# A Fourier filter and gated network on one core: the second transform stage as three products, with its input stored as a high and a low part

## The chip, the cores and the metric

The kernel runs on one core of a Trainium2 chip. The metric is the device time of one execution in microseconds (us). One core has TensorE (PE, matrix products), VectorE (DVE), ScalarE (ACT), GpSimd (POOL) and SyncE (SP, which here only issues transfers). PE, DVE, ACT, POOL and SP each work through a list of instructions in a fixed order; the order is the one in which the program was written.

## The reference

```python
X = np.fft.rfft(x, axis=1)                       # x: 8 x 3136 x 256
Y = X * (filt_r + 1j * filt_i)[None]
h0 = np.fft.irfft(Y, n=3136, axis=1)
h = np.maximum(h0 @ w_in, 0)                     # 256 -> 1024
c = sum(conv_w[k] * shift(h, k - 1) for k in range(3))   # three taps along the sequence
out = (h * sigmoid(c)) @ w_out                   # 1024 -> 256
```

All of it in fp32; the weights w_in, conv_w and w_out come as float64 bits and are turned into fp32 on the chip.

## The kernel before

**Arithmetic.** A matrix product with fp32 operands can be written as one fp32 matmul, or as three matmuls of the type fp32r on operands that were split into a rounded high part and a low remainder: high by high, high by low, low by high. The helper `mm3` (L186 to L189) writes the three. The network's products (`inner`, `project`) are such triples; the Fourier transforms use single fp32 matmuls.

**Transforms.** 3136 = 112 x 28. A batch goes through four stages, each in 14 pieces q of two columns (112 or 120 partitions x 512 values). Stage "1" (`by_column`, L245) reads x, multiplies by a table `tab`, and its result goes through a copy of ACT (`store`, L240, tile `st`) to DRAM, `a_dram`. Stage "2" (`second`, L249, L252 for q = 13) reads `a_dram` back in another order into a tile `tin` and multiplies by the constant `s2_sb`; `filt` then multiplies by the filter on DVE (L264 to L266) and adds on POOL (L267). Stage "3" (L249 again, input `z`) multiplies by `s3_sb` and goes through ACT and `st` to `b_dram`. Stage "4" (L275) reads `b_dram` into `tin`; DVE and ACT write it to the network's input `y`, ACT the high part (L156), POOL the low part (L162).

**Loop.** Batch 0 is transformed by other code in the first 86 us. Then comes the main loop over slots m: 8 slots (NF) make a unit of 510 tokens, and 48 slots make about a batch. In each slot, in this order of writing: every eighth time the finished output of a unit is copied out by DVE (`evacuate`, L549; counted within a batch of slots these are slots 6, 14, 22, 30, 38 and 46); `from_bank` for the transforms of the slot before; `want_in`, which issues input loads on SP; `transform` for this slot's transforms; `inner` (six 512-column matmuls, L187 to L189); ACT's relu, centre (L500), sigmoid, rounding; DVE's first tap (L504), gate (L510), second tap (L504); POOL's remainder of the gate (`rest_g`, L162); `project` (twelve 256-column matmuls, L536 to L538). ACT's centre writes one of four `t` buffers, which POOL's remainder frees.

**Plan of the transforms.** A table built ahead (`plan`) says which transforms stand in which slot. Counted from its own start, the t-th stretch of 48 slots (t = 1 to 7) holds stages "2", "3" and "4" of batch t and stage "1" of batch t + 1. The first stretch is special: slots 0 to 5 hold two "1" each, those of batch 1 that are still missing. From the second stretch on, "2" stands in slots 2, 3, 5, 7, 9, 11, 12, 14, 16, 18, 20, 21, 23, 25, "3" three slots after its "2", "1" in slots 0, 1, 4, 6, 8, 10, 13, 22, 27, 29 to 32 and 45, and "4" in slots 33 to 44, two of them in 33 and 39. The last stretch has no "1".

**Buffers and queue.** Two PSUM banks (`ps_t`) are shared by all transforms of the loop, in turn, so that a transform waits until the transform before the last has left its bank. A bank is left when ACT has copied it ("1", "3"), when DVE's `filt` has read it ("2"), or when DVE has copied it ("4"). `tin` has five buffers for all kinds of input, `st` three. `want_in` runs up to five inputs ahead. SP issues nearly all transfers: for each slot the stores of the slot before, then new loads of `tin`, then tables and filters.

Of the kernel before, what the change touches and what calls it, by code (L numbers as in the profile page):

```python
# [9 lines left out]
F32 = mybir.dt.float32  # L10
# [8 lines left out]
N2 = 28  # L19
G = 28  # L20
# [112 lines left out]
def tile_fft_filter_gated_ffn(  # L133
# [57 lines left out]
    dram = ctx.enter_context(tc.tile_pool(name="dram", bufs=1, space=bass.MemoryType.DRAM))  # L191
    a_dram = [dram.tile([N2, 112, D], F32, name=f"a_dram{b}") for b in range(B)]
    b_dram = [dram.tile([N2, 112, D], F32, name=f"b_dram{b}") for b in range(B)]
    a_out = [t[:].rearrange("n p d -> p n d") for t in a_dram]
    a_in = [t[:].rearrange("n (r g) d -> (n r) g d", g=G) for t in a_dram]
    b_out = [t[:].rearrange("n (r g) d -> (n r) g d", g=G) for t in b_dram]
# [5 lines left out]
    s2_sb = wc.tile([112, 120], F32, name="s2_sb")  # L202
    s2s_sb = wc.tile([112, 120], F32, name="s2s_sb")
    s3_sb = wc.tile([120, 112], F32, name="s3_sb")
    s3s_sb = wc.tile([120, 112], F32, name="s3s_sb")
    one_sb = wc.tile([128, 128], F32, name="one_sb")
    cw = wc.tile([128, 3, NF], F32, name="cw")
# [24 lines left out]

    def load_in(pool, kind, b, q, bufs, tag):
        r = pool.tile([112, 2, D], F32, name=tag, bufs=bufs)
        nc.sync.dma_start(out=r, in_={"1": xv, "2": a_in, "4": b_in}[kind][b][:, pair(q)])
        return r

    def store(pool, kind, b, q, ps, bufs, tag, queue=nc.sync):
        st = pool.tile([112, 2, D], F32, name=tag, bufs=bufs)
        nc.scalar.activation(st, ps[0:112].rearrange("p (j d) -> p j d", d=D), AF.Copy)  # L240
        queue.dma_start(out={"1": a_out, "3": b_out}[kind][b][:, pair(q)], in_=st)

# [11 lines left out]
    def second(ps, q, r):  # L254
        by_row(ps[0:120], q, r, s2_sb, s2s_sb)

    def third(ps, q, z):
# [27 lines left out]
    def load_weights(k, pool):  # L285
        raws[k] = raw = pool.tile([128, 2, 1024], I32, name="raw", bufs=1 if pool is tp else 2)
        for part, w in enumerate((w_in, w_out)):
            nc.sync.dma_start(out=raw[:, part], in_=w[:, 1024 * k:1024 * k + 1024])
# [6 lines left out]

    def convert(k, pool, n=2):

        for j in range(2):
            em = pool.tile([128, 2, 2, 256], I32, name="em", bufs=n)
            w = pool.tile([128, 2, 256], F32, name="ws", bufs=n)  # L300
            yield from to_f32(w, raws[k][:, :, 512 * j:512 * j + 512], em[:, 0], em[:, 1])
# [10 lines left out]
    with (  # L312
# [3 lines left out]
    ):  # L316
        fts, tabs, rows, zs, pss = {}, {}, {}, {}, {}
        by_r = [sc.tile([120, 4, N2], F32, name=f"by_r{i}", bufs=1) for i in range(2)]
        bt = sc.tile([128, KT, G, 112], F32, name="bt", bufs=1)
# [31 lines left out]
        with tc.tile_pool(name="sq", bufs=2) as sq:  # L351
# [15 lines left out]
            def first_loads(c):  # L367
                table("1", c)
                r = sq.tile([128, 4, D], F32, name="rows", bufs=5)
                nc.sync.dma_start(out=r, in_=xt[0:128, 4 * c:4 * c + 4])  # L370
# [24 lines left out]
            for i in range(NP + 4):  # L395
# [6 lines left out]
                if 0 <= i - NP < AHEAD:  # L402
                    ps = bank()
                    by_column(ps, tab("1", i - NP), rows.pop(("1", i - NP)))
                    store(tp, "1", 1, i - NP, ps, 3, "st", nc.scalar)
                if 0 <= i - 4 < NP:
# [7 lines left out]
                if i == 5:  # L414
                    table("1", 0)
                    for q in range(AHEAD):
                        r = sq.tile([128, 2, D], F32, name="xa", bufs=2)
                        nc.sync.dma_start(out=r, in_=xt[N1:N1 + 128, pair(q)])
# [33 lines left out]
    ts, hs, gs, pos, joined = {}, {}, {}, {}, {}  # L452
    ring = [[wp.tile([128, UO + 66], F32R, name=f"g{i}{h}", bufs=1) for h in range(2)] for i in range(4)]
    for pair_of in ring:
# [176 lines left out]
    def transform(op):  # L631
# [20 lines left out]
    def from_bank(op):  # L652

        kind, b, q = op
        ps = banks.pop(op)
        if kind in "13":
            store(tp, kind, b, q, ps, 3, "st")
            stored[kind, b] = stored.get((kind, b), 0) + 1
# [15 lines left out]
    with tc.manual_schedule(engines=COMPUTE | {mybir.EngineType.SP}):  # L674
# [3 lines left out]
        want_filter(0)  # L678
        late = convert(3, wp, 1)
        for m in range(NF * NU + PLAG + 1):  # L680
            p1, p2, p3, p4, p6, p7 = (at(m - k) for k in (1, 2, 3, 4, PLAG, PLAG + 1))
            new, old = plan.get(m, []), plan.get(m - 1, [])
            if p7:
                evacuate(*p7)
            for op in old:
                from_bank(op)
# [73 lines left out]
```

## Time and profile before

| | |
|---|---|
| median of 3 runs | 1554.89 us (1553.32 to 1556.66) |
| the profiled execution | 1554.59 us |
| its span in the profile | 1552.8 us |
| busy: PE, DVE, ACT, POOL | 98%, 76%, 74%, 53% of the span |
| moved by DMA | 229.49 MB, mean 148 GB/s |

Line numbers (L249) are those of the kernel before. "Idle before, releaser" in a group of instructions is the time in which the engine stood still ahead of them, and what it was waiting for. An fp32 matmul counts as several instructions of PE ("x2" for one piece of stage "2"). Ends of matmuls are modelled; the distance from one start to the next tells their cost better than their busy time. The chain of waits gives each step the time to the next step.

### The profile page before, as it was taken

The numbers are of one execution on the slowest core, as the hardware profiler recorded it, in microseconds if no ns is written. First come the engines' busy times: TensorE is split into PE (matmuls) and PEld (weight loads), VectorE is DVE, ScalarE is ACT, GpSimd is POOL, SyncE is SP. The second block draws the span as 40 slices with busy tenths as digits, with TensorE's granted clock in tenths as the row PEclk, the third lists the DMA queues.
The fourth block names the chain that finished last, engine by engine and source line by source line (L and its number), as shares of the span: only waits on it lengthen the run. The fifth ranks groups of instructions, "written<-read, shape, count | busy, mean of one in ns | idle before, by whom it ended". The sixth has DMA issues, their size and how long they took to land.

```text
span 1552.8 us, 26446 instructions
## 1 busy us (share of the span) xinstructions
PE 1519.7 (98%) x9202; PEld 1290.6 (83%) x9202; DVE 1185.3 (76%) x1810; ACT 1144.7 (74%) x1973; POOL 828.3 (53%) x721
## 2 busy tenths in 40 slices
PE   6999999999999999999999999999999999999999
PEld 5777788877997789877898778987799878999998
DVE  7978766788677877778777776778867888777776
ACT  3576668766896668866787667976688667888886
POOL 4644447545574555645565445744557445664444
PEclk9999999999999999999999999999999999999999
DMA  8867653665436555465544665356543543300000
GB/s 302 256 185 215 208 170 109 181 200 166 135 110 202 179 155 159 121 193 169 177 124 143 185 196 153 97 179 203 165 135 100 160 140 110 101 28 15 28 28 30
DMA packets 158436, 229.49 MB, mean 148 GB/s; under 512 B 16432, under 2 KB 109088, under 8 KB 158304
## 3 DMA queue, kind: packets, MB, share of 16 engines
q1 hardware_dynamic: 157824, 227.35, 48.4%
q8 instruction: 73, 1.20, 0.3%
q14 instruction: 59, 0.48, 0.1%
q10 hardware_dynamic: 480, 0.46, 0.1%
HBM read 157.10 MB, written 70.65 MB: 147 GB/s over the span
## 4 chain that ended last, share of the span: by engine, by line
PE 92%; DVE 2%; ACT 2%; DMA 2%; issue 2%; SPq 0%; POOL 0%; ACTq 0%; POOLq 0%; DVEq 0%
PE ps_h L187 12%; PE ps_h L189 12%; PE ps_h L188 12%; PE po L536 12%; PE po L538 12%; PE po L537 11%; PE ps_t L249 10%; PE ps_t L275 6%; PE ps_t L245 5%; DMA rows<-in_x 1%; PE ps_t L252 1%; ACT br L346 0%; DVE v L265 0%; DVE z L264 0%; DMA f<-in_filt 0%
## 5 line engine op out<-in xcount | busy, mean ns | idle before, releaser
L504 DVE SCALAR_TENSOR_TENSOR t<-ps_h,cw,t 128x510 f32<-128x510 f32 (+1 forms) x800 | 589.1, 737 | 301.5 <-ACT t L500 298.4
L162 POOL TENSOR_TENSOR g<-t,g 128x510 fp32r<-128x510 f32 (+1 forms) x400 | 505.3, 1273 | 203.6 <-ACT g L156 191.9
L536 PE MATMUL po<-wo,g 128*128 128x256 f32 (+1 forms) x1576 | 440.4, 279 | 0.1
L538 PE MATMUL po<-wo,g 128*128 128x256 f32 (+1 forms) x1576 | 439.5, 279 | 0.0
L537 PE MATMUL po<-wo,g 128*128 128x256 f32 (+1 forms) x1576 | 439.3, 279 | 0.0
L495 ACT ACTIVATE ps_h<-ps_h 128x512 f32<-128x512 f32 (+1 forms) x400 | 234.7, 587 | 243.9 <-PE ps_h L189 242.2
L500 ACT ACTIVATE t<-ps_h,cw 128x510 f32<-128x510 f32 (+1 forms) x400 | 272.4, 681 | 102.8 <-POOL g L162 70.1
L267 POOL TENSOR_TENSOR z<-z,v 120x512 f32<-120x512 f32 x112 | 144.8, 1293 | 380.4 <-DVE v L266 312.7
L187 PE MATMUL ps_h<-y,wi 128*128 128x512 f32 (+1 forms) x688 | 333.4, 485 | 0.5 <-DVE y L159 0.5
L536 PEld LDWEIGHTS po<-wo,g 128*128 128x128 f32 (+1 forms) x1576 | 297.0, 188 | 17.3 <-ACT g L156 0.3
L537 PEld LDWEIGHTS po<-wo,g 128*128 128x128 f32 (+1 forms) x1576 | 296.4, 188 | 17.0
L538 PEld LDWEIGHTS po<-wo,g 128*128 128x128 f32 (+1 forms) x1576 | 296.6, 188 | 0.6 <-POOL g L162 0.5
L189 PE MATMUL ps_h<-y,wi 128*128 128x512 f32 (+1 forms) x688 | 270.1, 393 | 0.0
L188 PE MATMUL ps_h<-y,wi 128*128 128x512 f32 (+1 forms) x688 | 270.1, 393 | 0.0
L510 DVE TENSOR_TENSOR t<-ps_h,t 128x510 f32<-128x510 f32 (+1 forms) x400 | 268.6, 671 | 0.9 <-ACT t L507 0.8
L507 ACT ACTIVATE t<-t 128x510 f32<-128x510 f32 (+1 forms) x400 | 245.3, 613 | 1.7 <-DVE t L504 1.6
L156 ACT ACTIVATE g<-t 128x510 fp32r<-128x510 f32 (+1 forms) x400 | 245.1, 613 | 0.2 <-DVE t L510 0.2
L162 POOL TENSOR_TENSOR y<-z,y 128x448 fp32r<-128x448 f32 x98 | 138.5, 1422 | 93.8 <-ACT y L156 91.9
L187 PEld LDWEIGHTS ps_h<-y,wi 128*128 128x128 f32 x688 | 130.4, 189 | 44.3 <-issue 23.6
L188 PEld LDWEIGHTS ps_h<-y,wi 128*128 128x128 f32 x688 | 130.7, 190 | 41.3 <-issue 24.3
L189 PEld LDWEIGHTS ps_h<-y,wi 128*128 128x128 f32 x688 | 130.0, 189 | 30.2 <-POOL wi L162 0.3
L240 ACT ACTIVATE st<-ps_t 112x512 f32<-112x512 f32 x194 | 114.0, 590 | 11.2 <-PE ps_t L245 11.1
(91 smaller groups left out, 1608.0 us busy)
## 6 DMA issues: line engine op xcount, KB each, us to landing
filt<-in_filt SPq DMA_DIRECT2D x98, 512.0 KB
tin<-a_dram SPq DMA_DIRECT2D x98, 224.0 KB
b_dram<-st SPq DMA_DIRECT2D x98, 224.0 KB
tin<-b_dram SPq DMA_DIRECT2D x98, 224.0 KB
tin<-in_x SPq DMA_DIRECT2D x96, 224.0 KB
a_dram<-st SPq DMA_DIRECT2D x96, 224.0 KB
out<-ot SPq DMA_DIRECT2D x45, 256.0 KB
tab<-in_m SPq DMA_DIRECT2D x98, 98.0 KB
```

What stands on the lines that cost most here:

```text
L156: nc.scalar.activation(dst, src, AF.Copy)
L162: nc.gpsimd.tensor_tensor(out=dst, in0=src, in1=hi.bitcast(F32), op=ALU.subtract)
L187: nc.tensor.matmul(ps, lhsT=wh, rhs=rh, start=start, stop=False, **kw)
L188: nc.tensor.matmul(ps, lhsT=wh, rhs=rl, start=False, stop=False, **kw)
L189: nc.tensor.matmul(ps, lhsT=wl, rhs=rh, start=False, stop=stop, **kw)
L500: nc.scalar.activation(t, hs[u, f][:, 1:n + 1], AF.Copy, scale=cw[:, 1, f:f + 1])
L504: nc.vector.scalar_tensor_tensor(out=t, in0=h[:, k:place(u)[2] + k], scalar=cw[:, k, f:f + 1], in1=t, op0=ALU.mult, op1=ALU.add)
L507: nc.scalar.activation(ts[u, f], ts[u, f], AF.Sigmoid)
L510: nc.vector.tensor_mul(ts[u, f], hs.pop((u, f))[:, 1:place(u)[2] + 1], ts[u, f])
L536: nc.tensor.matmul(o, lhsT=gh[:, c:c + n], rhs=wo[0][:, f], start=first, stop=False, skip_group_check=True)
L537: nc.tensor.matmul(o, lhsT=gh[:, c:c + n], rhs=wo[1][:, f], start=False, stop=False, skip_group_check=True)
L538: nc.tensor.matmul(o, lhsT=gl[:, c:c + n], rhs=wo[0][:, f], start=False, stop=last, skip_group_check=True)
```

## The change

**Stage "2" of batches 2 to 7 becomes a triple.** The constants `s2_sb` and `s2s_sb` are split once, at slot 8, by POOL, into `second_parts` (tiles `s20`, `s21`, `s2s0`, `s2s1`). `second_split` runs `mm3` on them. Batch 1 keeps the single fp32 matmul.

**Stage "1" of batches 2 to 7 stores two parts.** ACT writes the rounded high part to the tile `sh`, as it wrote `st`; DVE then subtracts it from the bank and writes the low part right behind (L159, 112 x 512). Both go to DRAM, the low part to a new tensor `r_dram`, and are loaded back by two loads for each piece of stage "2", into the two halves of a tile `tia`. That makes 84 subtractions, 84 more stores and 84 more loads of 224 KB.

**Buffers.** `tin` (now for "1" and "4" only) has three buffers instead of five; `tia` (stage "2") has three, twice as large; `st` (stage "3") two instead of three; `sh` (stage "1") two. `want_in` runs up to six inputs ahead, but has at most three of stage "2" and three of the others loaded and unused. The `rows` tiles of batch 0 have four buffers instead of five, and the last quarter of the weights passes through buffers of `tia` and `st`. The network's `ring` tiles are narrower by 64 columns that nothing uses.

```diff
-    def load_in(pool, kind, b, q, bufs, tag):
-        r = pool.tile([112, 2, D], F32, name=tag, bufs=bufs)
-        nc.sync.dma_start(out=r, in_={"1": xv, "2": a_in, "4": b_in}[kind][b][:, pair(q)])
+    def load_in(pool, kind, b, q):
...
+        if kind == "2":
+            r = pool.tile([112, 2, 2, D], F32R, name="tia", bufs=3)
+            for h, t in enumerate((a_in, r_in)):
+                nc.sync.dma_start(out=r[:, h].bitcast(F32), in_=t[b][:, pair(q)])
+            return r
+        r = pool.tile([128, 2, D], F32, name="tin", bufs=3)[0:112]
+        nc.sync.dma_start(out=r, in_={"1": xv, "4": b_in}[kind][b][:, pair(q)])
         return r
...
+    def store_first(pool, b, q, ps, queue=nc.sync):
+
+        st = pool.tile([112, 2, 2, D], F32R, name="sh", bufs=2)
+        p = ps[0:112].rearrange("p (j d) -> p j d", d=D)
+        hi_act(st[:, 0] if b > 1 else st[:, 0].bitcast(F32), p)
+        queue.dma_start(out=a_out[b][:, pair(q)], in_=st[:, 0].bitcast(F32))
+        if b > 1:
+            lo_dve(st[:, 1], p, st[:, 0])
+            queue.dma_start(out=r_out[b][:, pair(q)], in_=st[:, 1].bitcast(F32))
...
+    def second_split(ps, q, r):
+
+        if q < NP - 1:
+            mm3(ps[0:120], *second_parts[0], *(r[:, h].rearrange("p j d -> p (j d)") for h in range(2)))
+        else:
+            for j, parts in enumerate(second_parts):
+                mm3(ps[0:120, j * D:j * D + D], *parts, r[:, 0, j], r[:, 1, j])
...
     def want_in():
-        while wanted["in"] < min(done["in"] + 5, len(inputs)) and ready(inputs[wanted["in"]]):
+        while wanted["in"] < min(done["in"] + 6, len(inputs)) and ready(inputs[wanted["in"]]):
             op = inputs[wanted["in"]]
+            if sum((o[0] == "2") == (op[0] == "2") for o in got_in) == 3:
+                break
             wanted["in"] += 1
-            got_in[op] = load_in(tp, *op, 5, "tin")
+            got_in[op] = load_in(tp, *op)
...
-            second(ps, q, r)
+            (second_split if b > 1 else second)(ps, q, r)
```

The order on SP at the start of the loop. Before: five loads of `tin` stand ahead of the loop; then (after four tables of batch 0, `in_m2g`) each slot has two stores, two loads of `tin`, two tables.

```order
L235 DMA tin<-in_x 112x512 x5
L623 DMA tab<-in_s 112x224 x3
L628 DMA filt<-in_filt 128x1024
L623 DMA tab<-in_s 112x224
L357 DMA tab_704<-in_m2g 112x448
L357 DMA tab_736<-in_m2g 112x448
L357 DMA tab_772<-in_m2g 112x448
L357 DMA tab_802<-in_m2g 112x448
L623 DMA tab<-in_s 112x224
L241 DMA a_dram_58<-st 112x2x256 x2
L235 DMA tin<-in_x 112x512 x2
L623 DMA tab<-in_s 112x224 x2
```

Now (the lines of the changed kernel have other numbers: L245 is the load, L253 the store, L665 the table):

```order
L245 DMA tin<-in_x 112x512 x3
L665 DMA tab<-in_s 112x224 x3
L670 DMA filt<-in_filt 128x1024
L665 DMA tab<-in_s 112x224
L397 DMA tab_719<-in_m2g 112x448
L397 DMA tab_751<-in_m2g 112x448
L397 DMA tab_787<-in_m2g 112x448
L397 DMA tab_817<-in_m2g 112x448
L665 DMA tab<-in_s 112x224
L253 DMA a_dram_58<-sh 112x2x256 x2
L245 DMA tin<-in_x 112x512 x2
L665 DMA tab<-in_s 112x224 x2
```

Three loads stand ahead of the loop instead of five. The rows of a slot read alike, but its two loads are now those of the second "1" of this slot and the first of the next, where before they were those of the second "1" of the next slot and the first of the slot after it.

The order on PE in slot 23 of the second stretch, where a "3" (input `z`) and a "2" stand one behind the other. Before:

```order
L538 MATMUL po_3867<-wo_86,g_902 128x256
L249 MATMUL ps_t<-z,s_sb 112x512
L249 MATMUL ps_t<-tin,s_sb 120x512
L187 MATMUL ps_h<-y_2436,wi_84 128x512
L188 MATMUL ps_h<-y_2437,wi_84 128x512
L189 MATMUL ps_h<-y_2436,wi_85 128x512
```

Now (L269 is the single matmul, L187 to L189 on `ps_t` the triple; `s_86` and `s_87` are the high and the low part of `s2_sb`):

```order
L269 MATMUL ps_t<-z,s_sb 112x512
L187 MATMUL ps_t<-tia,s_86 120x512
L188 MATMUL ps_t<-tia,s_86 120x512
L189 MATMUL ps_t<-tia,s_87 120x512
L187 MATMUL ps_h<-y_2476,wi_95 128x512
L188 MATMUL ps_h<-y_2477,wi_95 128x512
```

The single fp32 row of the "2" became three rows; nothing else moved.

The order on DVE at the same place: the last operations of slot 22, then those of slots 23 and 24. Before:

```order
L504 SCALAR_TENSOR_TENSOR t<-ps_h,cw,t 128x510
L510 TENSOR_TENSOR t<-ps_h,t 128x510
L504 SCALAR_TENSOR_TENSOR t<-ps_h,cw,t 128x510 x2
L510 TENSOR_TENSOR t<-ps_h,t 128x510
L504 SCALAR_TENSOR_TENSOR t<-ps_h,cw,t 128x510
L264 TENSOR_TENSOR z<-ps_t,filt 120x512
```

Now (L544 the taps, L550 the gate, L292 the filter):

```order
L544 SCALAR_TENSOR_TENSOR t<-ps_h,cw,t 128x510
L550 TENSOR_TENSOR t<-ps_h,t 128x510
L544 SCALAR_TENSOR_TENSOR t<-ps_h,cw,t 128x510
L159 TENSOR_TENSOR sh<-ps_t,sh 112x512
L544 SCALAR_TENSOR_TENSOR t<-ps_h,cw,t 128x510
L550 TENSOR_TENSOR t<-ps_h,t 128x510
L544 SCALAR_TENSOR_TENSOR t<-ps_h,cw,t 128x510
L292 TENSOR_TENSOR z<-ps_t,filt 120x512
```

The subtraction for the "1" of slot 22 stands between the second tap of slot 22 and the first tap of slot 23.

More of the change, by code (lines that the diff above doesn't have):

```diff
@@ L192, in tile_fft_filter_gated_ffn @@
     a_dram = [dram.tile([N2, 112, D], F32, name=f"a_dram{b}") for b in range(B)]
+    r_dram = [dram.tile([N2, 112, D], F32, name=f"r_dram{b}") for b in range(B)]
     b_dram = [dram.tile([N2, 112, D], F32, name=f"b_dram{b}") for b in range(B)]
-    a_out = [t[:].rearrange("n p d -> p n d") for t in a_dram]
-    a_in = [t[:].rearrange("n (r g) d -> (n r) g d", g=G) for t in a_dram]
+    a_out, r_out = ([t[:].rearrange("n p d -> p n d") for t in ts] for ts in (a_dram, r_dram))
+    a_in, r_in = ([t[:].rearrange("n (r g) d -> (n r) g d", g=G) for t in ts] for ts in (a_dram, r_dram))
     b_out = [t[:].rearrange("n (r g) d -> (n r) g d", g=G) for t in b_dram]
@@ L203, in tile_fft_filter_gated_ffn @@
     s2s_sb = wc.tile([112, 120], F32, name="s2s_sb")
+    second_parts = [[wc.tile([112, 120], F32R, name=f"{n}{h}") for h in range(2)] for n in ("s2", "s2s")]
     s3_sb = wc.tile([120, 112], F32, name="s3_sb")
     s3s_sb = wc.tile([120, 112], F32, name="s3s_sb")
-    one_sb = wc.tile([128, 128], F32, name="one_sb")
     cw = wc.tile([128, 3, NF], F32, name="cw")
@@ L285, in load_weights @@
     def load_weights(k, pool):
-        raws[k] = raw = pool.tile([128, 2, 1024], I32, name="raw", bufs=1 if pool is tp else 2)
+        if pool is tp:
+            raws[k] = [pool.tile([128, 2, 2, D], F32R, name="tia", bufs=3).rearrange("p a j d -> p a (j d)").bitcast(I32) for _ in range(2)]
+            for j in range(2):
+                for part, w in enumerate((w_in, w_out)):
+                    nc.sync.dma_start(out=raws[k][j][:, part], in_=w[:, 1024 * k + 512 * j:1024 * k + 512 * j + 512])
+            return
+        raws[k] = raw = pool.tile([128, 2, 1024], I32, name="raw", bufs=2)
         for part, w in enumerate((w_in, w_out)):
@@ L294, in convert_conv, with convert @@
         yield from to_f32(cw.rearrange("p (o k) f -> p o (k f)", o=1), conv_raw, e, m)
[L296 removed]
+    def convert(k, pool):
         for j in range(2):
[L299 to L301 removed]
+            if pool is tp:
+                if j == 0:
+                    em = pool.tile([128, 2, 2, D], F32R, name="tia", bufs=3).bitcast(I32)
+                w, raw = pool.tile([128, 2, D], F32, name="st", bufs=2), raws[k][j]
+            else:
+                em = pool.tile([128, 2, 2, 256], I32, name="em", bufs=2)
+                w, raw = pool.tile([128, 2, 256], F32, name="ws", bufs=2), raws[k][:, :, 512 * j:512 * j + 512]
+            yield from to_f32(w, raw, em[:, 0], em[:, 1])
             halves = [(t[0][:, j, 256 * k:256 * k + 256], t[1][:, 2 * k + j]) for t in zip(wi, wo)]
@@ L368, in first_loads @@
                 table("1", c)
-                r = sq.tile([128, 4, D], F32, name="rows", bufs=5)
+                r = sq.tile([128, 4, D], F32, name="rows", bufs=4)
                 nc.sync.dma_start(out=r, in_=xt[0:128, 4 * c:4 * c + 4])
@@ L416, in tile_fft_filter_gated_ffn @@
                     for q in range(AHEAD):
-                        r = sq.tile([128, 2, D], F32, name="xa", bufs=2)
+                        r = tp.tile([128, 2, D], F32, name="tin", bufs=3)
                         nc.sync.dma_start(out=r, in_=xt[N1:N1 + 128, pair(q)])
@@ L452, in tile_fft_filter_gated_ffn @@
     ts, hs, gs, pos, joined = {}, {}, {}, {}, {}
-    ring = [[wp.tile([128, UO + 66], F32R, name=f"g{i}{h}", bufs=1) for h in range(2)] for i in range(4)]
+    ring = [[wp.tile([128, UO + 2], F32R, name=f"g{i}{h}", bufs=1) for h in range(2)] for i in range(4)]
     for pair_of in ring:
@@ L655, in from_bank @@
         ps = banks.pop(op)
+        if kind == "1":
+            store_first(tp, b, q, ps)
+        if kind == "3":
+            store_third(tp, b, q, ps)
         if kind in "13":
-            store(tp, kind, b, q, ps, 3, "st")
             stored[kind, b] = stored.get((kind, b), 0) + 1
@@ L678, in tile_fft_filter_gated_ffn @@
         want_filter(0)
-        late = convert(3, wp, 1)
+        late = convert(3, tp)
         for m in range(NF * NU + PLAG + 1):
@@ L684, in tile_fft_filter_gated_ffn @@
                 evacuate(*p7)
+            if m == NF:
+                for (h, l), t in zip(second_parts, (s2_sb, s2s_sb)):
+                    nc.gpsimd.tensor_copy(h, t)
+                    lo_pool(l, t, h)
             for op in old:
```

13 lines of the change are left out of this document (9 added, 4 removed).

## The prediction

> **What bounds the kernel now.** I read the page first (busy shares, then the chain of waits), then the windows along the span, then PE's groups, and last the timelines of the places that the change touches.
>
> ```profile
> span 1552.8 us, 26446 instructions
> PE 1519.7 (98%) x9202; PEld 1290.6 (83%) x9202; DVE 1185.3 (76%) x1810; ACT 1144.7 (74%) x1973; POOL 828.3 (53%) x721
> PE 92%; DVE 2%; ACT 2%; DMA 2%; issue 2%; SPq 0%; POOL 0%; ACTq 0%; POOLq 0%; DVEq 0%
> ...
> 86.00:109.00 23.00, 20.64 (x93) 15.74 (x92) 18.75 (x31) 17.74 (x32) 6.68 (x14) 1.00 0.84 247
> 400.00:600.00 200.00, 199.03 (x1199) 169.12 (x1197) 148.96 (x228) 148.70 (x254) 104.88 (x91) 1.00 0.55 164
> 1200.00:1300.00 100.00, 97.42 (x528) 76.75 (x527) 81.78 (x124) 65.01 (x117) 49.23 (x39) 0.98 0.48 145
> ```
>
> The first two lines are the busy shares, the third the chain; in the windows the columns after the length are PE, PEld, DVE, ACT, POOL, then the granted clock (1.00), DMA's share and GB/s. PE is busy 199.03 of 200 us in the middle of the loop and makes 92% of the chain: a microsecond taken from PE is worth a microsecond, as long as no other engine was about to be late anyway. Two places differ. From 86 to 109 us, the first six slots of the loop, PE is busy only 20.64 of 23 us and the DMA engines are busy 0.84 of the time, far above the 0.55 of the middle: there transfers decide. And from 1200 to 1300 us, where batch 7 has its stages "2" and "3" and no stage "1" fills PE, 2.6 us are idle: another engine is the limit.
>
> The execution profiled took 1554.59 us, 1.8 us of it outside the span, and lies 0.3 us under the median, so one sum serves for both. Differences under 0.2% (3.1 us) I call the same; that is about what a measurement of this kernel can tell.
>
> **Part 1: the triple on PE.** The chain gives each step's time to the next start.
>
> ```profile
> 359.81 0.86 PE ps_t L249 x2
> 360.67 0.24 PE ps_h L187
> 360.91 0.23 PE ps_h L188
> 361.14 0.23 PE ps_h L189
> 362.07 0.12 PE po L536
> ```
>
> One fp32 piece of 512 columns takes 0.86 us, one fp32r matmul of 512 columns 0.23, of 256 columns 0.12. So a triple takes 3 x 0.23 = 0.70 us (for q = 13 six of 256 columns, 6 x 0.12 = 0.70 as well) and saves 0.16 to 0.17 us. With 14 pieces in each of batches 2 to 7, 84 x 0.17 = 14.3 us. That is the whole that can be won, if PE may start its next work that much earlier each time. The split of the constants at slot 8 is four small POOL operations, once, on an engine idle almost half of its time: nothing.
>
> **Does PE get the saving?** Stage "2" is followed by DVE's filter, and there a loop closes.
>
> ```profile
> 354.75 0.68 DVE L264 TENSOR_TENSOR z<-ps_t,filt 120x512 f32<-120x512 f32 x1
> 358.17 2.52 POOL L162 TENSOR_TENSOR g<-t,g 128x510 fp32r<-128x510 f32 x2
> 359.50 0.69 ACT L500 ACTIVATE t<-ps_h,cw 128x510 f32<-128x510 f32 x1 [0.49 <-POOL g L162]
> 360.22 0.75 DVE L504 SCALAR_TENSOR_TENSOR t<-ps_h,cw,t 128x510 f32<-128x510 f32 x1 [1.35 <-ACT t L500]
> 362.14 0.68 DVE L264 TENSOR_TENSOR z<-ps_t,filt 120x512 f32<-120x512 f32 x1
> 363.32 1.03 PE L249 MATMUL ps_t<-z,s_sb 120*112 120x512 f32 x2
> 364.32 1.09 PE L249 MATMUL ps_t<-tin,s_sb 112*120 112x512 f32 x2
> ```
>
> The filter (from 354.75) delays POOL, which has to add for it before it takes the gate's remainders (358.17); ACT's centre waits for the `t` buffer that POOL frees (0.49 us of idle time, releaser POOL); DVE's first tap waits 1.35 us for ACT; three DVE operations later the next filter starts, at 362.14. From filter to filter that is 7.39 us for two slots. The "3" at 363.32 and the "2" at 364.32 lie 1.00 us apart instead of the 0.86 of a piece: the "2" waits for the filter of the bank before, which ends near 364.2. So in the stretch of a batch where a "2" comes every other slot, PE is already held to the pace of this loop, and a shorter "2" only makes it wait longer. I count as kept about six of a batch's fourteen: the first few, before the loop has closed, and the last two, after which three slots have neither "2" nor filter. That is 6 x 0.17 = 1.0 us for each of batches 2 to 6, and five pieces, 0.85 us, in batch 7. Bounds: nothing kept, and all 14.3 us kept.
>
> **Part 2: the subtraction on DVE.** This operation is not in the loop of before. Its nearest rows:
>
> ```profile
> L264 DVE TENSOR_TENSOR z<-ps_t,filt 120x512 f32<-120x512 f32 x98 | 66.9, 683 | 1.3 <-DMA filt<-in_filt 1.1
> L159 DVE TENSOR_TENSOR y<-ps,y 128x448 fp32r<-128x448 f32 x14 | 13.8, 1030 | 1.1 <-ACT y L156 1.0
> ```
>
> L264 reads a PSUM bank and one SBUF tile over 512 values in 0.683 us. L159 is the same helper, but writes in strides, 1.03 us. The new one writes contiguous values, so I take 0.69 us; the ends are 0.68 and 1.03. 84 of them make 58 us of DVE on 1185 busy us. In its place in the order it stands ahead of the first tap, where DVE has 1.35 us of idle time waiting for ACT; that covers it, unless ACT's centre comes at once, which is the case when no filter precedes. What it does change is the release of the bank. A "1" used to leave its bank with ACT's copy; now it leaves with DVE's subtraction, behind DVE's second tap of the slot before.
>
> ```profile
> 371.68 1.02 PE L249 MATMUL ps_t<-z,s_sb 120*112 120x512 f32 x2
> 372.22 0.74 DVE L504 SCALAR_TENSOR_TENSOR t<-ps_h,cw,t 128x510 f32<-128x510 f32 x1
> 372.54 1.02 PE L249 MATMUL ps_t<-tin,s_sb 112*120 112x512 f32 x2
> 336.33 1.40 DVE L549 COPY ot<-po 128x512 f32<-128x512 f32 x2 [0.97 <-PE po L538]
> 337.70 1.02 PE L249 MATMUL ps_t<-tin,s_sb 112*120 112x512 f32 x2
> ```
>
> Slot 23 of the stretch: the tap runs to about 372.9, the subtraction to 373.6, and PE wants the bank for the "2" at 372.54: 1.0 us of waiting. Behind the waiting "2" on PE stand the next `inner` and `project`, so the wait is on the path. Slot 14: the two copies of a finished unit end near 337.65, the subtraction near 338.35, PE wants the bank at 337.70: 0.65 us. In slots 5, 8, 10 and 12 a "3" or another piece stands between, and there is room. From the two waits I take off what the loop of part 1 would have made PE wait anyway, about 0.7 us, and put 0.93 us on each of five stretches. Batches 2 to 6 then come to 5 x (0.93 - 1.0), about -0.4 us; with batch 7, -1.2. The ends: 0 and 1.65 us a stretch, 0 to 8 in all. In the first stretch the same waits come in places where PE waits already.
>
> **Part 3: three `tin` buffers at the start of the loop.** This is the largest term.
>
> ```profile
> 86.46 1.89 PE L245 MATMUL ps_t<-tin,tab 112*112 112x256 f32 x8
> 88.39 0.60 ACT L240 ACTIVATE st<-ps_t 112x512 f32<-112x512 f32 x1 [0.27 <-PE ps_t L245]
> 88.15 1.19 SPq L241 DMA_DIRECT2D a_dram<-st  x2
> 89.39 0.95 SPq L235 DMA_DIRECT2D tin<-in_x  x2
> 94.52 3.92 DMA tab<-in_s
> 98.58 1.09 PE L245 MATMUL ps_t<-tin,tab 112*112 112x256 f32 x4 [0.96 <-DMA tab<-in_s]
> 102.23 1.09 PE L245 MATMUL ps_t<-tin,tab 112*112 112x256 f32 x4 [0.30 <-issue]
> 106.18 1.09 PE L245 MATMUL ps_t<-tin,tab 112*112 112x256 f32 x4 [0.60 <-ACT t L500]
> 108.50 1.03 PE L245 MATMUL ps_t<-tin,tab 112*112 112x256 f32 x4
> ```
>
> The second "1" of a slot is at 98.58 (slot 3), 102.23 and 106.18 (slot 5), about 3.8 us apart; slot 6 begins at 108.50. In between, the chain ran through a table that took 3.92 us from its issue at 94.52: a load here lands some 3.9 us after it is issued.
>
> By the order on SP, the second "1" of slot m + 1 now gets its data from a load that is issued only in that slot, behind the stores of slot m. So a cycle closes: second "1" from 87.4 (86.46 and half of 1.89), ACT's copy 88.39 to 88.99, second store to 89.34, load issued at 89.39, landed at 89.39 + 3.92 = 93.3. That is 5.9 us from one second "1" to the next, against 3.8 before. Five of them: 93.3, then four times 5.9, 116.9 in slot 5, where it was 106.18: +10.7 us. But a slot that lasts longer asks for its 1.12 MB (two stores, two loads of 229 kB, two tables of 100 kB) at 1.12 MB / 5.4 us = 207 GB/s instead of 247, so a load should land sooner; I take 3.4 us, a cycle of 5.4, 114.9, +8.7, in round numbers **+9 us**. Nothing after it gives this back, since afterwards PE has hardly any idle time to fill (1 us in 200 in the window above). Ends: at 2.4 us a load (halfway to the 0.93 us that 229 kB take at 247 GB/s) the cycle is 4.4, +4.7; with 0.4 us more for a later store, 6.3, +12.
>
> The Trainium skill, "DMA: Bandwidth & Descriptors", section "Latency and other measured facts", has a rule that speaks for the smaller value: a lighter load on the HBM makes the fixed part of a transfer shorter. Its section "Anatomy of one DMA" gives about 2.0 us plus bytes over 436 GB/s (for another queue), an estimate of 2.5 us for this load, which would make this term about +5 us instead of +9; the 3.92 us of the trace at 0.84 DMA share does not follow it.
>
> **Part 4: three `tin` buffers in stage "4".** Slot 39 of each stretch has two "4".
>
> ```profile
> 612.83 1.04 PE L275 MATMUL ps_t<-tab,tin 112*128 112x112 f32 x8
> 613.75 0.85 SPq L567 DMA_DIRECT2D out<-ot  x2
> 614.69 0.34 SPq L235 DMA_DIRECT2D tin<-b_dram  x1
> 616.47 1.94 PE L275 MATMUL ps_t<-tab,tin 112*128 112x112 f32 x16
> ```
>
> The load for the second "4" of slot 39 can be issued only after the "4" of 612.83, and SP has the stores of the finished unit in front of it, so its place is where a load stands now, at 614.69. At 2.8 to 3.4 us it lands at 617.5 to 618.1; PE wants it at 616.47 + 0.97 = 617.44. So 0 to 0.7 us, say 0.35, in each of six stretches: +2 us; ends 0 and 5.
>
> **The rest.** 84 more stores and 84 more loads make 38.5 MB on 229.49: the DMA share of the middle goes from 0.55 to about 0.65. `tia` loads have more than a slot and a half of lead with three buffers, and a filter load of 512 KB is wanted one "2" ahead, so 0; if transfers became late they would first show as DVE waiting for `filt`. Narrower rings, `rows` and the late weights: 0, since none of them sits where PE waits, but for four `rows` buffers in the first 20 us, up to +1.
>
> **Sum.** 1554.6 - 1.2 (parts 1 and 2) + 9 (part 3) + 2 (part 4) = 1564.4, say **1564 us**, 0.6% slower.
>
> **Rivals.**
> A, the saving arrives whole. The loop of part 1 may have slack that a single place does not show: PE idles only 1 us in 200. Then -14.3 stands against parts 3 and 4: 1554.6 - 14.3 + 11 = 1551, and 1546 with the low ends of part 3 (4.7) and part 4 (0). It decides as soon as the part kept exceeds parts 3 and 4 by 3.1 us. Against it: the 1.00 us between "3" and "2", and the window from 1200 us on, where PE waits though it has less to do.
> B, the start does not wait, because loads land in time: 1554.6 - 1.2 + 2 = 1555. Against it: the 3.92 us of the table.
> C, DVE becomes the bound. If the subtraction is not covered in slots 4 to 27, where seven "1" of a stretch lie, 7 x 0.69 = 4.8 us for each of five stretches, 24 us: 1588; if half is covered, 1576. For it: that loop is already as slow as PE. Against it: the 1.35 us of idle time ahead of the tap.
>
> **How the numbers follow.** My forecast (1564, by its own terms 1556 to 1572) has a chance of 0.57, A 0.16, B 0.12, C 0.15. Faster by over 0.2% is A, 0.16; the same is B and the lowest end of the forecast, 0.15; slower 0.69. The range reaches from most of A, 1549, to the half of C, 1577.
>
> **What would show it.** Right: the second "1" of slots 1 to 5 over 5 us apart, with waits for `tin` of in_x, and slot 6 near 117; stage "2" pieces 0.70 us long but the "3" and "2" of slot 21 still one filter apart; waits of PE for DVE's L159 in slots 14 and 23 only. Wrong: slot 6 near 109 (B), a stretch of 48 slots shorter by 2 us or more (A) or longer by 2 us or more (C), or DVE waiting for `filt`. The forecast rests most on the time of a load at the start, and on how much of 14.3 us the loop swallows.

## The result and the profile after

The changed kernel takes 1574.12 us (median of 4 runs, 1573.57 to 1575.99) against 1555.05 us before: a ratio of 1.0122, 95% interval 1.0106 to 1.0138. The direction of the forecast was right, the size was not: 1564 was forecast, +9.5 us, and it became +19. The page of the changed kernel, then windows along its span (columns as before):

```profile
span 1572.4 us, 26964 instructions
PE 1516.2 (96%) x9292; PEld 1305.6 (83%) x9292; DVE 1235.4 (79%) x1894; ACT 1149.8 (73%) x1973; POOL 830.1 (53%) x725
PE 83%; DVE 5%; DMA 4%; ACT 3%; issue 2%; SPq 1%; POOL 1%; POOLq 0%; ACTq 0%; DVEq 0%
...
86.00:109.00 23.00, 15.73 (x73) 11.88 (x71) 12.01 (x19) 12.45 (x21) 4.13 (x11) 0.93 0.49 145
400.00:600.00 200.00, 196.69 (x1197) 169.41 (x1196) 157.85 (x243) 149.63 (x256) 108.30 (x91) 1.00 0.64 189
```

PE is now busy 15.73 of 23 us at the start (20.64 before) and 196.69 of 200 in the middle (199.03). PE's share of the chain fell from 92% to 83%. PE's busy time fell by only 3.5 us, and that says little, because ends of matmuls are modelled. The waits of PE from 200 us on, with total, times and longest:

```profile
PE ps_t L187 <- PE ps_t L269: 5.1, 11, 0.6
PE ps_t L187 <- DVE sh L159: 4.9, 6, 0.9
PE ps_t L265 <- ACT st L260: 3.6, 5, 0.7
PE ps_t L187 <- issue: 2.8, 1, 2.8
PE ps_t L303 <- DMA tin<-b_dram: 2.6, 6, 0.9
```

Before, the list had ACT's 3.6 us, 2.2 us once in the last stretch (the row of 2.8 us here) and rows of at most 1.4. New are the first two rows, the triples (L187 on `ps_t`) that wait for a bank, and the last, stage "4" (L303) that waits for its load. Of the eleven waits of the first row five stand in slot 14 and six in slot 21; of the six of the second row five stand in slot 23 and one in slot 5.

Where the 19 us lie is seen best from the starts of PE's matmuls, which both traces have for all 400 slots. The table gives the first `inner` matmul of a slot, after minus before:

```
slot 0                                  +3.35
within slots 0 to 5                    +10.43
rest of the first stretch               -1.24
stretches 2 to 6    +1.78 +1.19 +1.38 +1.29 +1.42, together +7.06
stretch 7                               -0.35
stretches 8 and 9                       +0.21
sum                                    +19.46
```

Three further executions of this kernel (e13, and e4 and e14, where only the late conversion starts one slot later) give +10.8 to +12.0 us for slots 0 to 5 and +6.1 to +7.8 for stretches 2 to 6, so this profile is no exception there.

The start, as forecast: second "1" of a slot at 91.44 in slot 0 and 119.94 in slot 5, five cycles of 5.70 us on average (5.4 forecast, 3.8 before).

```profile
97.02 1.09 PE L265 MATMUL ps_t<-tin,tab 112*112 112x256 f32 x4 [2.18 <-DMA tin<-in_x]
95.93 3.16 SPq L253 DMA_DIRECT2D a_dram<-sh  x2
99.14 0.92 SPq L245 DMA_DIRECT2D tin<-in_x  x2
102.74 2.02 PE L265 MATMUL ps_t<-tin,tab 112*112 112x256 f32 x4 [2.37 <-ACT sh L156]
119.94 1.09 PE L265 MATMUL ps_t<-tin,tab 112*112 112x256 f32 x4 [1.80 <-ACT g L156]
...
102.72:106.13 3.41, 3.39 (x8) 2.67 (x9) 1.72 (x4) 0.60 (x1) 2.51 (x4) 0.50 0.27 82
```

The second "1" of slot 1 waits 2.18 us for `tin`. SP then stands in the stores until 99.09, since the second of them needs ACT's copy of that "1"; only then does it issue the load at 99.14, which the next second "1" uses at 102.74. That one's wait is booked on ACT (2.37 us), which had been done since 101.85; it is the same load. The five loads of this kind are used 3.0 to 3.6 us after their issue, 3.4 on average, which is what I took.

One cycle is longer than the others: the third took 6.54 us, the rest 5.16 to 5.72. The last row shows why: from 102.72 to 106.13 us the granted clock was 0.50. The "1" at 102.74 ran for 2.02 us instead of 1.09, so its copy, its store and the next load came some 0.9 us later. All nine runs with this cycle have one to three such stretches between 95 and 123 us; the kernel before and e3, e5 and e10, which start like it, have none there.

Slots 14 and 23 of the second stretch:

```profile
349.79 0.68 DVE L159 TENSOR_TENSOR sh<-ps_t,sh 112x512 fp32r<-112x512 f32 x1
350.57 0.46 PE L187 MATMUL ps_t<-tia,s 112*120 112x512 f32 x1 [0.56 <-PE ps_t L269]
384.38 1.02 PE L269 MATMUL ps_t<-z,s_sb 120*112 120x512 f32 x2
384.92 0.74 DVE L544 SCALAR_TENSOR_TENSOR t<-ps_h,cw,t 128x510 f32<-128x510 f32 x1
385.58 0.68 DVE L159 TENSOR_TENSOR sh<-ps_t,sh 112x512 fp32r<-112x512 f32 x1
386.32 0.49 PE L187 MATMUL ps_t<-tia,s 112*120 112x512 f32 x1 [0.91 <-DVE sh L159]
```

The subtraction takes 0.68 us, as estimated. In slot 23 it ends at 386.26 and the triple starts at 386.32. It stands where the forecast put it: behind the second tap (384.92), in front of a "2" that PE wanted some 0.9 us sooner.

### The profile page after: what moved, and what is told of

The parts are those of the page before. It is cut to its first block, busy times and chain, and to the rows that moved or that the text cites. A ratio compares the mean times of both kernels' runs of the same rounds, so it can differ in the third digit from the quotient of the medians.

```text
span 1572.4 us, 26964 instructions
## 1 busy us (share of the span) xinstructions
PE 1516.2 (96%) x9292; PEld 1305.6 (83%) x9292; DVE 1235.4 (79%) x1894; ACT 1149.8 (73%) x1973; POOL 830.1 (53%) x725
## 4 chain that ended last, share of the span: by engine, by line
PE 83%; DVE 5%; DMA 4%; ACT 3%; issue 2%; SPq 1%; POOL 1%; POOLq 0%; ACTq 0%; DVEq 0%
PE ps_h L187 11%; PE ps_h L189 11%; PE ps_h L188 11%; PE po L576 11%; PE po L578 11%; PE po L577 11%; PE ps_t L303 5%; PE ps_t L269 5%; PE ps_t L265 5%; DMA tin<-b_dram 2%; PE ps_t L187 1%; PE ps_t L188 1%; PE ps_t L189 1%; DVE t L544 1%; DMA f<-in_filt 1%
## 5 line engine op out<-in xcount | busy, mean ns | idle before, releaser
L544 DVE SCALAR_TENSOR_TENSOR t<-ps_h,cw,t 128x510 f32<-128x510 f32 (+1 forms) x800 | 588.5, 736 | 269.4 <-ACT t L540 266.2
L187 PE MATMUL ps_h<-y,wi 128*128 128x512 f32 (+1 forms) x688 | 310.7, 452 | 0.0
L188 PE MATMUL ps_h<-y,wi 128*128 128x512 f32 (+1 forms) x688 | 270.3, 393 | 0.0
L189 PE MATMUL ps_h<-y,wi 128*128 128x512 f32 (+1 forms) x688 | 270.3, 393 | 0.0
L550 DVE TENSOR_TENSOR t<-ps_h,t 128x510 f32<-128x510 f32 (+1 forms) x400 | 268.6, 672 | 1.1 <-ACT t L547 0.8
L187 PEld LDWEIGHTS ps_h<-y,wi 128*128 128x128 f32 x688 | 130.5, 190 | 32.7 <-issue 10.4
L189 PEld LDWEIGHTS ps_h<-y,wi 128*128 128x128 f32 x688 | 130.2, 189 | 30.0
L265 PE MATMUL ps_t<-tin,tab 112*112 112x256 f32 x384 | 100.8, 385 | 16.9 <-ACT sh L156 4.5
```

The source lines that it names most:

```text
L187: nc.tensor.matmul(ps, lhsT=wh, rhs=rh, start=start, stop=False, **kw)
L188: nc.tensor.matmul(ps, lhsT=wh, rhs=rl, start=False, stop=False, **kw)
L189: nc.tensor.matmul(ps, lhsT=wl, rhs=rh, start=False, stop=stop, **kw)
L544: nc.vector.scalar_tensor_tensor(out=t, in0=h[:, k:place(u)[2] + k], scalar=cw[:, k, f:f + 1], in1=t, op0=ALU.mult, op1=ALU.add)
L550: nc.vector.tensor_mul(ts[u, f], hs.pop((u, f))[:, 1:place(u)[2] + 1], ts[u, f])
```

## The experiments

Steps of a slot are told below as the time from the first `project` matmul of the slot before to that of the slot itself, minus the same step of the kernel before. The kernel before took 1551.12 to 1560.15 us in these comparisons, so for a kernel with one execution I go by its steps and name its time only beside them.

**e1: memory for the loads of the start.**

```diff
+        if (kind, b) == ("1", 1) and q >= AHEAD + 3:
+            ...   # r = a piece of the idle y tile of the odd batches
+            nc.sync.dma_start(out=r, in_=xv[b][:, pair(q)])
+            return r
```

The edit of `want_in`, which lets these loads run up to five ahead, is left out here.

> The changed kernel, but the missing stage-1 inputs of batch 1 from the fourth on are loaded into memory that lies idle then (that of y for odd batches), up to five ahead as in the kernel before. Theory 1, the three tin buffers make each second "1" of slots 0 to 5 wait for a load of its own slot: these slots lose 2.5 us or less against the kernel before instead of 10.4, the time falls by 7 to 9 us, to 1565 to 1567. Rival: the transfers of the start are simply too many for the DMA engines, whatever the buffers: the loss in slots 0 to 5 stays above 7 us, 1571 or more.

1565.15 us. Slots 0 to 5 lose 2.65 us against the kernel before instead of 10.43.

```profile
89.75 3.73 PE L274 MATMUL ps_t<-tin,tab 112*112 112x256 f32 x8 [2.37 <-DMA tab<-in_s]
103.86 1.09 PE L274 MATMUL ps_t<-y,tab 112*112 112x256 f32 x4 [0.50 <-ACT t L549]
107.97 1.09 PE L274 MATMUL ps_t<-y,tab 112*112 112x256 f32 x4 [0.77 <-ACT t L549]
```

The second "1" of slots 3 and 4 is 4.1 us apart, and the mean of the five cycles is 4.26 us (5.70 in the changed kernel, 3.8 before). The same bytes moved, so it was the buffers, not the transfers as such. The 2.37 us for a table are new: in this kernel two loads stood ahead of the tables on SP, waiting for the memory to come free.

**e2: no subtraction.**

```diff
-            lo_dve(st[:, 1], p, st[:, 0])
-            queue.dma_start(out=r_out[b][:, pair(q)], in_=st[:, 1].bitcast(F32))
+            queue.dma_start(out=r_out[b][:, pair(q)], in_=st[:, 0].bitcast(F32))
```

> The changed kernel without the 84 subtractions on DVE; the second store writes the high part once more, so every transfer stays and the low part is left out. Theory 1, the bank that is released by DVE makes stage "2" wait in slots 14 and 23: the waits there fall from 0.85 and 1.22 us to the 0.40 that the last stretch shows, where there are no subtractions, about 1.3 us for each of five stretches, 1567 to 1568. Rival, the loop over filter, POOL, ACT and the taps swallows what the triple saves: the waits move to other slots of the stretch and the time stays within 1.5 us of 1574. Rival, the subtraction slows the whole DVE loop as well: waits in slots 5 and 21 fall too, 1564 or less.

1568.1 us. Slots 14 and 23 take 0.15 to 0.22 us less than in the kernel before, where the changed kernel takes 0.63 and 1.00 more: the subtraction costs some 0.8 and 1.2 us there. Stretches 3 to 6 come to -1.12, -0.44, -0.72 and -0.91 against +1.19 to +1.42, 2.1 us a stretch. The second stretch is no witness: one execution, with 3.56 us more in slot 21, behind two filter loads for which DVE waited 1.71 and 1.87 us. The third expectation (slots 5 and 21 too) came for slot 5, which has no wait left, but there e13 below hardly has one either, with the subtraction. Slot 21 stays as it was or gets worse, by 0.35 us on average in stretches 3 to 6. The triples' waits of this run from 200 us on, where no row for the subtraction is left:

```profile
PE ps_t L187 <- issue: 6.4, 3, 2.8
PE ps_t L187 <- PE ps_t L268: 1.8, 4, 0.5
```

All seven of them stand in slot 21, but for one of 2.84 us in slot 12 of the last stretch.

**e3 and e5: the triple alone, in the kernel before.**

```diff
-            second(ps, q, r)
+            (second_split if b > 1 else second)(ps, q, r)
```

Here `second_split` takes the one tile that is loaded for both data operands.

> The kernel before with stage "2" of batches 2 to 7 as three products, both data operands being the one tile that is loaded now, so that the low part of the data is left out: no subtraction, no further transfer, tin with five buffers; the rings are narrowed by their unused columns. It prices the triple by itself. If PE's saving arrives whole: 84 x 0.16 = 13 us less than the kernel before, 1541 to 1543. By the prediction's count (six pieces of fourteen): about 6 us, 1548 to 1550. If the last stretch of the changed kernel (0.35 us won, with 2.5 us of new waits) is the rule: 6 x 0.7, 1550 to 1552.

> The kernel before with stage "2" of batches 2 to 7 as three products, the data operands both being the one tile that is loaded now and the weights a slice of wi, so that the low part of the data and the true table are left out: no subtraction, no further transfer, every buffer and tile as before, the rings too (e3 had them narrower, and its project matmuls came every 117.9 ns instead of 114.7). If PE's saving arrives whole: 13 to 14 us less than the kernel before. By the prediction's count (six pieces of fourteen): about 6 us less. In the profile: 0.16 us less in each slot with a "2", given back, where it is given back, as a wait in slot 21.

e3, with narrow rings, came to 1552.52 us and decides nothing: its `project` matmuls start every 117.6 ns instead of 115.8 (means of 4312 intervals; the expectation above had 114.7 for the kernel before), and the last stretches, which hold no transform, are 2.1 us longer. e5 has every tile as before and took 1545.61 us. Its slots with a "2" are 0.08 to 0.22 us shorter, thirteen of the fourteen; the other is slot 21. Given back are 0.11 to 0.18 us in slot 8 and, in three stretches of five, 0.26 to 0.63 in slot 21:

```profile
PE ps_t L245 <- ACT st L240: 3.6, 5, 0.7
PE ps_t L187 <- PE ps_t L249: 2.8, 6, 0.8
PE ps_t L187 <- issue: 2.7, 1, 2.7
```

The stretches come to -1.19, -1.27, -2.23, -2.07, -1.65 and, without a "1", -0.99: together -9.4 us of the possible 13.7 (84 x 0.163).

**e4 and e14: the late conversion from slot 1.** The last quarter of the weights is converted by operations written into the first slots; in the changed kernel three of them stand on DVE ahead of the loop.

```diff
-            steps(late, 3 if m < 5 else 1)
+            steps(late, 3 if 0 < m < 6 else m > 0)
```

> The changed kernel with the conversion of the last quarter of the weights started in slot 1 instead of slot 0, which takes its first three DVE operations (1.48, 0.62 and 1.22 us in the trace of the changed kernel) out of the stretch of DVE work ahead of the loop. Theory: DVE is the bound from 10 to 90 us, so slot 0 begins about 2 us earlier than the 92.2 of the changed kernel, and the time falls by about 2 us, to 1572. Rival: the 3.35 us that slot 0 was late came from the first loads alone (first weights there at 10.0 instead of 8.8 us): slot 0 stays at 92, no change.

> The changed kernel again, beside e14 on the same chip: 1573 to 1575.

> e4 again, timed in rounds. If the three DVE operations of the late conversion ahead of the loop delay slot 0: 2 to 4 us below e13. If slot 0's lateness was only the scatter of the first loads: within 1 us of e13.

In e4 slot 0 came 4.7 us sooner than in the changed kernel, which looked like a proof. Timed four times each it was not: e13 took 1571.82 us (1570.49 to 1574.75), e14 1572.99 (1572.15 to 1574.8), and slot 0 came at +1.52 and +1.98 us against the kernel before. e4 and e14 are the same kernel and lie 3.3 us apart there; e10, which has the code of the kernel before up to the second stretch, has slot 0 at +3.83. So the time up to slot 0 scatters by some 4 us from execution to execution, and the 3.35 us of the first profile cannot be put down to the change. That none of them is the change's is not shown either: the seven executions with the changed kernel's code ahead of the loop lie at +1.52 to +3.35, those with the code of the kernel before at 0.00, 0.42 and 3.83 (e3, e5, e10). The gain of 2 to 4 us that was expected of the later conversion does not show.

**e6 and e11: the second transform behind inner.**

```diff
+            new = sorted(new, key=lambda o: o[0] == "3") if m >= NW and [o[0] for o in new] == ["3", "2"] else new
+            behind = new[1:] if at(m) and m >= NW and len(new) == 2 else []
-            for op in new:
+            for op in new[:len(new) - len(behind)]:
                 transform(op)
             if a := at(m):
                 inner(*a)
+            for op in behind:
+                transform(op)
```

> The changed kernel with another order on PE from the second stretch on: where a slot has two transforms, the second stands behind inner, and "2" ahead of "3". Nothing is left out. Theory 1, PE waits for banks that are released too late by 0.4 to 1.2 us, and 1.4 us of inner ahead of the wait hides it: the waits of slots 6, 8, 14, 21, 23, some 4 us of a stretch, go, about 3 us or more in each of six stretches, 1556 or less. Rival, the loop over filter, POOL, ACT and the taps is the limit of slots 2 to 28: the waits come back at other slots or other matmuls (inner waiting for a bank of ps_h), and less than 1.2 us a stretch is won, 1567 or more.

> e6 again, timed in rounds beside the kernel before: 1545 to 1547, ratio 0.993 to 0.995.

1545.55 us in one execution; in rounds 1544.91 (1543.71 to 1547.26), ratio 0.9937, interval 0.9922 to 0.9952. From this order alone the changed kernel is 27 to 29 us faster (e13 and the first result). Stretches 2 to 6 now stand at -2.8 to -4.1 us each. Waits of PE from 200 us on, all of them, then slot 23:

```profile
PE ps_t L269 <- DVE v L294: 2.5, 3, 1.7
PE ps_t L303 <- issue: 1.4, 1, 1.4
PE ps_t L269 <- ACT st L260: 0.6, 1, 0.6
...
380.40 0.40 PE L187 MATMUL ps_t<-tia,s 112*120 112x512 f32 x1
381.10 0.40 PE L187 MATMUL ps_h<-y,wi 128*128 128x512 f32 x1
381.59 0.68 DVE L159 TENSOR_TENSOR sh<-ps_t,sh 112x512 fp32r<-112x512 f32 x1
382.50 1.02 PE L269 MATMUL ps_t<-z,s_sb 120*112 120x512 f32 x2
```

The "2" takes a bank that has long been free, `inner` runs while DVE subtracts (until 382.27), and the "3" starts at 382.50 without waiting. The waits hardly came back elsewhere. The three for the filter (L294) are 0.43 us in slot 21 of the second stretch and 1.65 and 0.42 us in slots 12 and 21 of the last. So the loop over filter, POOL, ACT and the taps was not the limit of these slots, but for slot 21 of one stretch in five.

**e7: loads ahead of the output's stores on SP**, in slots that copy out a unit.

```diff
+            if p7 and p7[1] == NF - 1:
+                want_in()
             if p7:
                 evacuate(*p7)
```

> The changed kernel with want_in ahead of evacuate as well in the slots that copy out a unit, so that on SP the loads of these slots stand in front of the stores of the output. Theory: the load for the second "4" of slot 39 is held up by those stores; it is issued about 1.2 us sooner, and the wait of slot 39 (0.43 to 0.63 us in each of stretches 2 to 6) goes; that of slot 33 (0 to 1.15) stays: 2 to 3 us less, 1571 to 1572. Rival: the load waits for its buffer, not for SP: no change, 1574.

1572.3 us. The steps of slot 39, +0.29 to +0.62 in the changed kernel, are gone in stretches 2 to 7, so the load of slot 39 was held up by SP. Slot 33 keeps 0.15 to 0.73 in four of five, and slot 5 took up to 1.59 more, behind a filter load for which DVE waited 2.10 us, which gave part of it back. For slot 33 the chain of the changed kernel shows, in the fifth stretch:

```profile
974.22 0.41 SPq L245
974.68 0.87 SPq L665
975.65 0.39 SPq L253
976.12 0.47 SPq L256
976.69 4.23 DMA tin<-b_dram
981.06 1.00 PE ps_t L303 x7
```

The load takes 4.23 us, and ahead of it SP issues one transfer after the other. It is issued 0.60 us after the first `inner` matmul of slot 32; in e12 below, where slot 33 of this stretch loses only 0.23 us, 0.56 us ahead of that matmul. So SP has a part in slot 33 too, which the order of e7 does not take away.

**e12: the subtraction ahead of the copies of a unit.**

```diff
+            early_out = [op for op in old if op[0] == "1" and p7 and p7[1] == NF - 1 and m >= NW]
+            for op in early_out:
+                from_bank(op)
+            old_rest = [op for op in old if op not in early_out]
             if p7:
                 evacuate(*p7)
...
-            for op in old:
+            for op in old_rest:
                 from_bank(op)
```

> The changed kernel with the copy and subtraction of a "1" ahead of the copies of a finished unit in those slots that have both (14, 30 and 46). Nothing is left out. Theory: the bank of slot 13's "1" comes free about 1.3 us sooner, while DVE was idle waiting for PE, so the wait of slot 14 (0.85 us) goes and that of slot 23 (1.22) stays: 0.8 us for each of five stretches, 1570. Rival: the loop needs the time anyway and the wait moves on to slots 21 and 23: under 2 us.

1566.88 us, 5 to 7 less than the changed kernel (e13 and the first result). Slot 14 falls from +0.63 to between -0.12 and -0.23, slot 23 stays at +0.95 to +1.04, as expected. By the steps of stretches 2 to 6 it is 7.5 us less: 4.05 in slot 14, 2.1 in slot 33 and 1.35 in slot 5, whose wait e13 hardly has either. That slot 33 hardly waits any more was not expected: the stores of slot 29's "1" now stand ahead of the output's stores on SP in slot 30, and the load for slot 33 is issued sooner. That this is the reason I have not tried by itself.

**e8 and e9: the repairs together.** e8 is e1, e4, e6 and e7 in one; e9 puts the start's loads behind the tables on SP and uses the order of e6 from slot 8 of the first stretch on (`m >= NF` in place of `m >= NW`, not shown).

```diff
-        want_in()
+        for op in inputs[:3]:
+            wanted["in"] += 1
+            got_in[op] = load_in(tp, *op)
```

> The changed kernel with the edits of e1 (memory for the loads at the start), e4 (late conversion from slot 1), e6 and e7 together; nothing is left out. If the losses are independent: 1574 - 8 - 4 - 18 - 2 = 1542. If the loop over filter, POOL, ACT and the taps is the limit (e6 by its rival): 1574 - 8 - 4 - 5 - 2 = 1555, no better than the kernel before.

> e8 with two edits: the loads of the start go behind the tables on SP (in e8 the first two stood in front of them and PE waited 2.25 us for a table in slot 0), and the second transform stands behind inner already in the first stretch, from slot 8 on. Nothing is left out. If the losses are independent: 1542 less 3 to 4 us at slot 0 and less 2 to 3 us of the waits in slots 13, 15 and 22 of the first stretch, 1535 to 1537. If the start is limited by the transfers whatever their order: 1540 to 1542.

e8 took 1542.14 us; it lost 2.25 us in slot 0 to a table, as e1 had. e9 took 1536.85 us (1536.57 to 1536.92), ratio 0.9883 to the kernel before, interval 0.9868 to 0.9898: 18 us faster than the kernel before, 35 to 37 faster than the changed one, and at the value expected for independent losses. That the sums come out is partly luck: they count 4 us for the later conversion, for which e14 shows nothing, and 18 for the order, which brought 27 to 29.

```profile
span 1534.6 us, 26968 instructions
PE 1504.3 (98%) x9292; PEld 1304.5 (85%) x9292; DVE 1235.8 (81%) x1894; ACT 1146.0 (75%) x1973; POOL 830.7 (54%) x725
```

**e10: the same order in the kernel before.** The edit of e6 on the kernel before.

> The kernel before (stage "2" in fp32, no parts) with the second transform behind inner and "2" ahead of "3", from the second stretch on. It tells what the change itself is worth once no bank is waited for. Its waits in slots 6, 8, 21 (1.45 to 2.07 us a stretch) go: 5 x 1.7 and some 3 in the last stretch, 1543 to 1546, so that the triple would be worth about 13 us less what its loads and subtractions still cost. Rival: the time stays at 1550 or more, because without the triple PE does not get ahead of DVE's loop and the waits were the loop's.

1544.96 us (1542.79 to 1547.23), ratio 0.9931, interval 0.9914 to 0.9948. Stretches 2 to 6 win 8.2 us together; the changed kernel in that order (e11) wins 17.6 in them. With few waits for a bank left (1.2 us from 200 us on in e10, 3.2 in e11), the triple and all its traffic is worth 9.4 us in these five stretches, and what the changed kernel loses against it is the start: e11 and e10 take the same time because slots 0 to 5 of e11 cost 12 us.

## Why the prediction was half right

**Right: the start.** +9 was forecast for slots 0 to 5, +10.4 came; the cycle of copy, store, load that was read out of SP's order is the one in the trace, and e1 breaks it. The size of the load was right as well, 3.4 us, though I read 3.92 from a table of 98 KB, not from a load of x. What the sum put at nothing is the clock: the stretch at 0.50 made the third cycle some 0.9 us longer. On the rule on lighter loads from the Trainium skill, "DMA: Bandwidth & Descriptors", section "Latency and other measured facts": the window at the start moved 145 GB/s instead of 247, and the packets of the first load of a slot ended 2.4 to 2.8 us after its issue instead of 2.6 to 3.4, so the transfer did become shorter, on average by 0.6 us; the runs do not show whether in its fixed part. The 2.5 us worked out from the page would have given a cycle of 4.5 us, and 5.7 was measured.

**Right: the two places.** The subtraction's 0.68 us, and waits in slots 14 and 23 of 0.65 and 1.0 us; e2 gives 0.8 and 1.2.

**Wrong: "about six of a batch's fourteen".** The kept part of the triple was sized at 1.0 us a stretch; e5 measures 1.2 to 2.2, mean 1.7. I took one row, 1.00 us between a "3" and a "2", for the state of a whole stretch. That row is slot 21. Slot 12 has the same order ("2" in the slot before, then "3" and "2"), and in the kernel before its "3" and "2" lie 0.86 us apart, the time of a piece, in each of stretches 2 to 6:

```profile
328.63 1.02 PE L249 MATMUL ps_t<-z,s_sb 120*112 120x512 f32 x2
329.49 1.02 PE L249 MATMUL ps_t<-tin,s_sb 112*120 112x512 f32 x2
```

There the "2" waits for no filter, so PE was not at the pace of the loop in the first half of the stretch. In e5 the savings are kept one by one up to slot 20 except for slot 8, and slot 21 makes a stretch at most 0.63 us longer. In e6 slots 21 and 22 together are 0.21 to 0.83 us shorter than in the kernel before in four stretches of five and 0.27 longer in the second, so even there PE mostly waited for a bank and not for the pace of DVE.

**Wrong: taking off "what the loop of part 1 would have made PE wait anyway, about 0.7 us".** There was little to take off. In e2 PE runs through slots 14 and 23 without a wait, and slot 21 waits only 0.35 us more instead. With 2.1 us a stretch (e2, stretches 3 to 6) instead of 0.93, this is the largest mis-sized term. By the steps against e5, slots 14 and 23 cost 9.9 us over five stretches: the two waits as they were sized, 1.63 us a stretch, and the saving of the two triples that stand there. Slot 5, where the prediction saw room, adds 1.4 in this execution (0.15 in e13), and slot 21 waits 0.6 less: 10.7 us instead of 4.65.

**A sign that came: the filter loads.** DVE waiting for `filt` was named as a sign of being wrong. From 200 us on it does so four times, 2.0 us in all (twice, 1.1 us, before). Three of these waits stand in slot 3 of stretches 3, 4 and 6, ahead of the wait of slot 5; what they cost PE was not tried by itself.

**Wrong: the loads of stage "4".** 0.35 us a stretch was forecast, for slot 39. Slot 39 cost 0.35 to 0.62, and slot 33, which also has two "4" and stands behind four "1" in a row, was left out; its step is up to 1.14. The two steps add up to 4.8 us over stretches 2 to 6, not 1.75.

So a stretch came to -1.7 + 2.15 + 0.95 = +1.4 us instead of -1.0 + 0.93 + 0.35 = +0.3, and 7 us instead of 1.4 over five of them. It was luck that the error of the first term hid a good third of the errors of the other two. The rest, 3.35 us at slot 0 and -1.24 in the first stretch (a wait in slot 13 that was there before is gone), was not in the sum; how much of the first is scatter is open.

**The rivals.** A (the saving arrives whole) was no nearer to the truth of the triple than the forecast: 9.4 us by e5, of 13.7 possible and 5.85 forecast. And it left out the waits of slots 14 and 23, which take all of it. The window from 1200 us on, which I held against A, shows one place again: a wait of 2.17 us for the filter in slot 12, and right behind it 3.41 us at a granted clock of 0.50. (By its own terms A's low end is 1545, not 1546, and the half of C is 1576, where the range says 1577.) B did not come. C (DVE becomes the bound) is refuted by e6: with all subtractions in place and 1235 us of DVE work, PE waits for the filter only 2.5 us in all from 200 us on, 2.1 of them in the last stretch, which has no subtraction.

**Still open.** Why the time up to slot 0 scatters by 4 us, how much of the 3.35 us there is the change's, and whether the order on SP is the reason that slot 33 became free in e12.

## What to carry to other kernels

When an operation is added to the release of a buffer, look at each place where the next user stands right behind it, and count the whole wait: a limit elsewhere may be subtracted only where the trace shows that limit at that very place. Where the trace shows a short wait for a bank, look first whether work that needs other banks can stand between; here a few lines that move the second transform behind `inner` (1.4 us) bring 10 us in the kernel before, about as much as the change of arithmetic brings in that order (9.4 us). And when buffers are divided by kind, the phase that used them all for one kind has to be followed slot by slot.

## What the runs showed of the hardware

**Matmul cadence.** In e3 the `project` matmuls start every 117.6 ns on average instead of 115.8, with the same work; it has the rings 64 unused columns narrower and four small tiles more. In e5, with every tile as before, it is 116.0, and in the changed kernel, whose rings are as narrow but whose other tiles lie elsewhere, 115.8. So the place of tiles seems to matter; which tile, and why, is open.

**Starts behind an fp32 matmul.** In the second stretch of e6, where "3" moved behind `inner`, the steps of slots 14 and 15 read -0.56 and +0.42 us, and those of 23 and 24 -0.56 and +0.40, though each pair sums to the 0.14 to 0.16 us that the triple saves. In e10, where nothing is saved, they read -0.40 and +0.42, and -0.40 and +0.40. Steps should be measured between matmuls with like neighbours, or over several slots.

**The granted clock.** It stood at 0.50 for 3.41 us in the third cycle of the start and for 3.41 us from 1246.9 us on in the kernel before, where PE had just waited 2.17 us. A matmul of `inner` took 0.63 us there instead of 0.40.
